# Attention and hard-swish MLP on one core: q and k transposed side by side by DMA and set apart by VectorE, decay rows from DRAM for all pairs

## The chip, the cores and the metric

The kernel runs on one core of a Trainium2 chip. The metric is device time in microseconds (us). Before the change, three runs gave a median of 357.02 us (356.66 to 357.11).

## The reference

Attention with a cumulative decay over 8 batches, 8 heads, 576 tokens and a head size of 64, and then an MLP with a hard-swish over all 4608 tokens. Cut to what matters:

```python
def attn(q, k, v, s):                       # q, k, v: 8 x 8 x 576 x 64, s: 8 x 8 x 576
    scores = (1 / 8) * q @ k^T              # 8 = sqrt(64)
    cum = cumsum(maximum(s, 0), axis=-1)
    bias = -(cum[:, :, :, None] - cum[:, :, None, :])
    scores = where(above the diagonal, -1e9, scores + minimum(bias, 0))
    return softmax(scores) @ v

x = attn(...) as (batch, token) rows of 8 heads x 64          # 4608 x 512
h = x @ w_in                                                  # 512 -> 2048
out = (h * clip(h + 3, 0, 6) / 6) @ w_out                     # 2048 -> 512
```

## The kernel before, in words

**Pairs and slots.** The 64 heads are taken two at a time: 32 pairs (p), each with 1152 tokens (2 x 576, the constant W2), which are 9 blocks of 128 (NTR). Everything that a pair needs lies in one of three slots (NS = 3, slot p % 3): qkT holds the transposed q and k side by side, v_h the values in f16. Scores are made as keys x queries: one operand is a 128-column block of kT, the other a stretch of qT, and the contraction runs over 128 partitions. The first 64 are the head's dimensions. Partitions 64 to 67 carry the decay: rows of the cumulative sum, in three f16 pieces, so that the product adds cum of the key minus cum of the query. Partitions 68 to 127 are mask rows: groups of ten tokens, with a large negative number for keys in later groups. So the scores come out of one matmul with decay and most of the mask. ScalarE takes the exponential from PSUM into Pm (L358), GpSimd zeroes the triangles of the blocks on the diagonal (affine_select, L363), TensorE multiplies by v_h (attend, L438), and VectorE divides (L448, L450). x_transpose turns the result for the MLP, on TensorE for some pairs (L476 with the copy L484) and by a DMA transpose for most pairs from 8 on (L468).

**How q and k get into the slots.** Three ways, by pair:
- Pairs 0 to 4 (FIRST = 4): turn_first. GpSimd or ScalarE casts q and k into x0 next to their decay columns (L792), TensorE transposes 68 columns at a time (L798), a copy puts 68 rows into the slot (L804).
- Pairs 5 to 9 (up to PTD = 10): cast_qk casts on GpSimd (L243), transpose_group turns 5 and then 4 blocks on TensorE (L302) and VectorE copies q's and k's 64 rows (L317). The four decay rows come by load_aug (L236) from a DRAM scratch that store_aug wrote (L599, 10 heads). The mask rows stay in the slot from the pair before.
- Pairs 10 to 31: cast_columns on GpSimd builds xb with 18 blocks of 128 columns, 9 for q and 9 for k. Each block has 64 columns of the cast (L282), four decay columns (L285, L286) and 60 mask columns. transpose_dma turns all 18 blocks by one DMA transpose straight into the slot, all 128 partitions (L291). The mask columns of the two xb buffers are filled once (copy_columns, L253) from a constant that load_columns brings from DRAM (L249). The decay columns come from decay_columns (27 TensorE transposes, L261, and a VectorE copy, L269) and decay_order (four GpSimd copies, L276).

**Order.** The schedule is written by hand: each engine works through its instructions in program order and waits in place. SyncE issues nearly all DMAs: loads of q, k (L210) and v (L224, L228), load_aug, transposes and results (L565). GpSimd issues the weight loads. A small fence DMA (L898) holds pair 4's loads back until a chunk of w_out has landed.

The first 8 heads run by themselves. Then comes the first MLP block, and with it decay_scan, decay_rows (GpSimd, L149 to L155), store_aug, the fence and the loads of pairs 4, 5 and 6. second_pair runs pairs 4 to 8, with tasks of the MLP put between; it loads pair p + 3 and casts for pair p + 1, and for pair p + 2 from 10 on. Its flag early (p > FIRST + 2) decides whether the cast and the first transpose group of pair p + 1 come ahead of x_transpose and attend or behind. From pair 9 on, att_tasks lists a pair's tasks (loads; the scores banks of the even and the odd head, s0 and s1; casts; attends) with costs, and weave puts them between the MLP's tasks in proportion. Tasks of cost 0 ride along.

**PSUM.** The MLP's first matmul (m1, L508) fills a 512-column bank, ScalarE clips it from below into trl (L518), VectorE multiplies trl, clipped from above, with the bank into gT (L519). Only then is the bank free. m1 has two banks in turn (3 and 4), in block 1 also bank 5 for every third group, and the second matmul (m2, L551) mostly bank 5, emptied by VectorE (L563).

Of the kernel before, what the change touches and what calls it, by code (L numbers as in the profile page):

```python
# [10 lines left out]
F16 = mybir.dt.float16  # L11
# [5 lines left out]
def kernel(  # L17
# [10 lines left out]
    nc = tc.nc  # L28

    B, H, SEQ, D = q.shape  # L30
    NH = B * H
# [35 lines left out]
    def pair_of_banks(b):  # L67
# [12 lines left out]
        name="sums",  # L80
    )

    gran = np.arange(SEQ) // GRAN
    rows = np.arange(60)
    amask_np = np.ones((2, 64, SEQ), dtype=np.float16)
    amask_np[0, 4:64] = gran[None, :] == rows[:, None]
    amask_np[1, 4:64] = np.where(gran[None, :] < rows[:, None], -16384.0, 0.0)
    row = np.arange(W2).reshape(NTR, 128).T % SEQ
    xaug_np = np.concatenate([amask_np[1][:, row], amask_np[0][:, row]], axis=2)
    xaug_dram = nc.inline_tensor(  # L90
        np.ascontiguousarray(xaug_np.transpose(1, 2, 0)).reshape(128, 2 * NTR * 64),
        name="xaug",
    )

    NA = 2 * (PTD - COLS)
    aug_dram = nc.dram_tensor("aug_scratch", (2, 4, NA * SEQ), F16, kind="Internal").ap()

    fence_dram = nc.dram_tensor("fence", (1, 32), F16, kind="Internal").ap()

# [6 lines left out]
    v_f = cpool.tile([128, NS, 2, 5, D], F32, tag="c_vf")  # L106
    v_h = cpool.tile([128, NS, 2, 5, VS], F16, tag="c_vh")
    Pm = cpool.tile([128, NS, PW], F16, tag="c_P")
    xb = cpool.tile([128, 2, 2 * NTR, 128], F16, tag="c_xb")
    dec = cpool.tile([128, NTR, 3, NP], F16, tag="c_dec")  # L110
    dec_f = cpool.tile([128, 3, NTR * NH], F16, tag="c_decf")
    xT = cpool.tile([128, KC, NT + 64], F16, tag="c_xT")
    warm = cpool.tile([128, 512], F16, tag="c_warm")
    one = cpool.tile([128, 2], F16, tag="c_one")
# [21 lines left out]
    wrap = work.tile([NH, 3, 128], F16, tag="wrap", bufs=1)  # L136

    def decay_scan():
        nc.vector.tensor_scalar(
# [6 lines left out]
    def decay_rows():  # L146
        r1 = work.tile([NH, SEQ], F32, tag="s0", bufs=1)
        g = nc.gpsimd
        g.tensor_copy(out=kaug[:, 0, :], in_=c8)  # L149
        nc.scalar.activation(out=qaug, in_=c8, func=AF.Copy, scale=-1.0)  # L150
        g.tensor_tensor(out=r1, in0=c8, in1=kaug[:, 0, :], op=ALU.subtract)
        g.tensor_copy(out=kaug[:, 1, :], in_=r1)
        g.tensor_tensor(out=kaug[:, 2, :], in0=r1, in1=kaug[:, 1, :], op=ALU.subtract)
        g.tensor_copy(out=wrap[:, :, 0:64], in_=kaug[:, 0:3, 512:SEQ])
        g.tensor_copy(out=wrap[:, :, 64:128], in_=kaug[:, 0:3, 0:64])  # L155

    def select(view, pattern, base, step, fill, src=None):
        nc.gpsimd.affine_select(
# [73 lines left out]

    def load_aug(p, eng):
        sl = p % NS
        c0 = (p - COLS) * W2
        eng.dma_start(  # L236
            out=qkT[64:68, sl, 0:2 * W2].rearrange("r (i c) -> r i c", i=2),
            in_=aug_dram[:, :, c0:c0 + W2].rearrange("i r c -> r i c"),
        )
# [3 lines left out]
        nc.gpsimd.tensor_copy(out=t, in_=qk_f.pop(p))  # L243
        qk_h[p] = t

    xaug = cpool.tile([128, 2 * NTR, 64], F16, tag="c_xaug")

    def load_columns():
        nc.sync.dma_start(out=xaug.rearrange("p t c -> p (t c)"), in_=xaug_dram.ap())  # L249

    def copy_columns(i, half):
        t = slice(half * NTR, (half + 1) * NTR)
        nc.vector.tensor_copy(out=xb[:, i, t, 64:128], in_=xaug[:, t, :])  # L253

    def decay_columns():
        pD = f16(pair_of_banks(6), 3 * NTR * NH)
        for i in range(3):
            for t in range(NTR):
                n = i * NTR + t
                c = 128 * t if t < 4 else 64 + 128 * (t - 5)  # L260
                nc.tensor.matmul(  # L261
                    out=pD[:, n * NH:(n + 1) * NH],
                    lhsT=wrap[:, i, :] if t == 4 else kaug[:, i, c:c + 128],
                    rhs=ident[0:NH, 0:NH],
                    is_transpose=True,
                    start=(n % 16 == 0),
                    stop=(n % 16 == 15 or n == 3 * NTR - 1),
                )
        nc.vector.tensor_copy(out=dec_f.rearrange("p i c -> p (i c)"), in_=pD)  # L269

    def decay_order():
        dv = dec_f.rearrange("p i (t a h) -> p t i a h", t=NTR, h=2)
        for r0, r1, j0, j1, h in (
            (0, 128, 0, 4, 0), (0, 64, 4, 5, 0), (64, 128, 4, 5, 1), (0, 128, 5, 9, 1)
        ):
            nc.gpsimd.tensor_copy(  # L276
                out=dec[r0:r1, j0:j1, :, :], in_=dv[r0:r1, j0:j1, :, :, h]
            )

    def cast_columns(p):  # L280
        x = xb[:, p % 2]
        nc.gpsimd.tensor_copy(  # L282
            out=x.rearrange("p (i t) c -> p t i c", i=2)[:, :, :, 0:D], in_=qk_f.pop(p)
        )
        nc.gpsimd.tensor_copy(out=x[:, NTR:2 * NTR, D:D + 3], in_=dec[:, :, :, p])  # L285
        nc.gpsimd.tensor_scalar_mul(  # L286
            out=x[:, 0:NTR, D + 3:D + 4], in0=dec[:, :, 0:1, p], scalar1=-1.0
        )

    def transpose_dma(p):  # L290
        nc.sync.dma_start(  # L291
            out=qkT[:, p % NS, 0:2 * W2].rearrange("p (t c) -> p t c", c=128),
            in_=xb[:, p % 2].rearrange("p t c -> p (t c)"),
            transpose=True,
        )

    def cast_v(p):
        sl = p % NS
# [315 lines left out]
    def att_tasks(p):  # L614


        more = p + 1 < NP

        def loads():
            if p + 3 < NP:  # L620
                load_pair(p + 3)
            if p < PTD - 1:
                cast_qk(p + 1)

        def casts():
# [12 lines left out]
        late = [(lambda: attend(2 * p - 1), 600 if PTD <= p < PTD + 3 else 1200)]  # L638
        back = []
        if p > FIRST:  # L640
            back = [(lambda: x_transpose(p - 1), 0 if by_dma(p - 1) else 640)]
        a = [(loads, 0)]
        if p <= PXD:
            a += scores(2 * p) + tr[0] + late
            a += scores(2 * p + 1) + [(casts, 0)] + tr[1] + back
        else:
            s0, s1 = scores(2 * p), scores(2 * p + 1)
            a = late + (back + a if by_dma(p - 1) else a + s0[:2] + back)
            a += (s0 if by_dma(p - 1) else s0[2:]) + tr[0]
            if p == PXD + 1:  # L650
                for half in range(2):
                    s1.insert(2 * half, (lambda half=half: copy_columns(1, half), 0))
            a += s1 + [(casts, 0)] + tr[1]
        return a, [(lambda: attend(2 * p), 1800 if PTD <= p + 1 < PTD + 3 else 1200)]

    def second_pair(p, fill):
        s0, s1, v = scores(2 * p), scores(2 * p + 1), values(2 * p)
        first = p == FIRST

        def more(n=1):  # L660
            run(fill[:n])
# [36 lines left out]
        if p + 3 < PTD:  # L698
            load_aug(p + 3, nc.sync)
        cast_v(p + 1)  # L700
        if PTD <= p + 2:
            cast_columns(p + 2)
            transpose_dma(p + 2)
        more()

# [269 lines left out]
```

## Time and profile before

| | |
|---|---|
| timed runs | 357.02 us median (356.66 to 357.11) |
| profiled execution, whole | 358.79 us |
| its span, first to last instruction | 357.0 us |
| granted TensorE clock | 1.00 |
| VectorE L519, 144 of 128x512 | 98.0 us, 686 ns each |
| TensorE L508 and L551, 512 columns | 143.3 and 138.9 us, 379 ns each |
| TensorE L261, decay transposes | 27 instructions |
| GpSimd L282, L285, L286, 22 each | 1147, 227 and 281 ns each |
| DMA transposes qkT<-xb, 22 | 4.7 us to landing (median), 2.8 us on SyncE |
| DMA transposes xT<-xs, 18 | 2.6 us to landing (median), 1.24 us on SyncE |
| store aug_scratch<-aug | 1, 90.0 KB |
| load xaug<-xaug | 1, 288.0 KB |
| loads qkT<-aug_scratch | 5, 18.0 KB each |

How to read it: busy time is what an engine's instructions cover; the idle time before a group of instructions is put down to what came last. A wait counts for the kernel only if TensorE, which is never long without work here, waits in the end. In the timeline, a row starts with start and duration in us, and xN counts like instructions merged into it; SPq is SyncE's queue of DMA issues.

### The profile page before, as it was taken

Reading aid. Unit: us, or ns where it says so; the run is one execution under the profiler, and the core shown is the slowest. Engines: PE = TensorE matmul, PEld = TensorE weight load, DVE = VectorE, ACT = ScalarE, POOL = GpSimd, SP = SyncE. Lnnn points to the kernel's source line nnn. Section 1 sums busy time; section 2 is a strip of 40 time slices with the busy share of each in tenths; the row PEclk is TensorE's granted clock in tenths of the full one; section 3 lists DMA queues with packets and bytes.
Section 4 is the critical chain, followed back from the end, with each engine's and each line's share of the span. In section 5 each row is a group of like instructions: output and inputs, shape, how many; then the busy total and the mean of one; then the engine's idle time right before and its main releaser. Section 6 shows DMA issues by size and latency. Waiting matters only on the chain.

```text
span 357.0 us, 7691 instructions
## 1 busy us (share of the span) xinstructions
PE 347.0 (97%) x2858; PEld 202.0 (57%) x2858; DVE 183.2 (51%) x314; ACT 208.0 (58%) x391; POOL 153.9 (43%) x371
## 2 busy tenths in 40 slices
PE   7999999999999999999999999999999999999995
PEld 3775566666555565655555555555555545444444
DVE  4758647787424563455345543544255635644531
ACT  4766456678646784777467755776478614534400
POOL 7695367754654555554445544454553200000000
PEclk9999999999999999999999999999999999999999
DMA  8999989899999999999998999999947110000012
GB/s 184 209 184 215 224 201 221 210 223 190 206 202 242 195 190 236 228 207 194 198 249 175 205 202 219 169 209 209 219 84 116 51 59 30 31 29 29 32 67 80
DMA packets 185389, 59.12 MB, mean 166 GB/s; under 512 B 177616, under 2 KB 180128, under 8 KB 185352
## 3 DMA queue, kind: packets, MB, share of 16 engines
q1 hardware_dynamic: 181720, 54.06, 70.2%
q0 software_dynamic: 2688, 4.19, 6.6%
q8 instruction: 22, 0.36, 0.4%
q10 hardware_dynamic: 944, 0.39, 0.4%
q14 instruction: 15, 0.12, 0.1%
HBM read 37.36 MB, written 9.53 MB: 131 GB/s over the span
## 4 chain that ended last, share of the span: by engine, by line
PE 82%; DMA 8%; DVE 3%; POOL 2%; ACT 1%; issue 1%; SPq 1%; POOLq 0%
PE PS L508 34%; PE PS L551 31%; PE PS L351 9%; PE PS L438 6%; DMA qkf<-in_k_dram 4%; DMA w_in<-in_moe_w_in_dram 2%; DMA qkT<-xb 2%; DVE qkT L317 1%; PE PS L574 1%; DVE gT L519 1%; ACT trl L518 1%; PE PS L476 1%; SPq L210 1%; POOL t L243 1%; POOL gT L792 1%
## 5 line engine op out<-in xcount | busy, mean ns | idle before, releaser
L519 DVE SCALAR_TENSOR_TENSOR gT<-trl,PS 128x512 f16<-128x512 f32 x144 | 98.0, 686 | 97.1 <-ACT trl L518 96.7
L508 PE MATMUL PS<-xT,w_in 128*128 128x512 f16 x576 | 143.3, 379 | 1.3 <-DVE gT L519 0.7
L518 ACT ACTIVATE trl<-PS,bias 128x512 f32<-128x512 f32 x144 | 98.7, 693 | 75.0 <-PE PS L508 73.2
L551 PE MATMUL PS<-w_out_sb,gT 128*128 128x512 f16 x560 | 138.9, 379 | 0.5 <-DVE osb L563 0.5
L358 ACT ACTIVATE Pm<-PS 128x384 f16<-128x384 f32 x224 | 102.7, 507 | 49.0 <-PE PS L351 46.8
L363 POOL TENSOR_SCALAR_AFFINE_SELECT Pm<-Pm 128x256 f16<-128x256 f16 x224 | 68.6, 308 | 109.3 <-ACT Pm L358 101.4
L508 PEld LDWEIGHTS <-w_in 128*128 128x128 f16 x576 | 60.9, 113 | 46.8 <-issue 2.4
L551 PEld LDWEIGHTS <-gT 128*128 128x128 f16 x560 | 51.4, 98 | 48.5 <-issue 0.7
L351 PE MATMUL PS<-qkT 128*128 128x256 f16 x392 | 61.8, 261 | 0.8 <-DMA qkT<-xb 0.6
L351 PEld LDWEIGHTS <-qkT 128*128 128x128 f16 x392 | 35.7, 98 | 31.3 <-DVE qkT L317 1.7
L438 PEld LDWEIGHTS <-Pm 128*128 128x128 f16 x960 | 37.5, 97 | 10.8 <-issue 0.3
L563 DVE TENSOR_SCALAR osb<-PS 128x512 f32<-128x512 f32 x35 | 24.1, 689 | 36.0 <-PE PS L551 35.8
L438 PE MATMUL PS<-v_h,Pm 128*128 128x65 f16 x960 | 40.4, 193 | 0.2
L450 DVE TENSOR_TENSOR xs<-PS,r 128x640 f16<-128x640 f32 x32 | 26.4, 825 | 1.1
L282 POOL CAST xb<-qkf 128x1152 f16<-128x1152 f32 x22 | 25.2, 1147 | 1.2 <-DMA qkf<-in_k_dram 1.2
L299 POOL CAST v_h<-v_f 128x640 f16<-128x640 f32 x32 | 23.0, 719 | 3.6 <-DMA v_f<-in_v_dram 3.5
L422 ACT ACTIVATE Pm<-PS 128x896 f16<-128x896 f32 (+1 forms) x16 | 13.1, 836 | 4.7 <-PE PS L416 4.6
L317 DVE COPY qkT<-PS 64x640 f16<-64x640 f16 (+1 forms) x20 | 9.1, 454 | 7.3 <-PE PS L302 7.0
L448 DVE RECIPROCAL r<-PS 128x10 f32<-128x10 f32 x32 | 6.9, 217 | 8.7 <-PE PS L438 8.3
L804 DVE COPY qkT<-PS 68x1152 f16<-68x1152 f16 (+2 forms) x13 | 7.5, 588 | 6.2 <-PE PS L798 6.1
L484 DVE COPY xT<-PS 128x576 f16<-128x576 f16 x14 | 6.4, 456 | 7.2 <-PE PS L476 6.0
L416 PE MATMUL PS<-qkT 128*128 128x64 f16 (+4 forms) x48 | 9.0, 277 | 0.6 <-DVE qkT L804 0.4
(74 smaller groups left out, 118.1 us busy)
## 6 DMA issues: line engine op xcount, KB each, us to landing
out_dram<-osb SPq DMA_DIRECT2D x35, 256.0 KB, 2.4
qkf<-in_q_dram SPq DMA_DIRECT2D x31, 288.0 KB, 3.3
qkf<-in_k_dram SPq DMA_DIRECT2D x31, 288.0 KB, 3.8
v_f<-in_v_dram SPq DMA_DIRECT2D x64, 128.0 KB, 3.4
w_in<-in_moe_w_in_dram POOLq DMA_DIRECT2D x4, 512.0 KB, 9.3
w_out_sb<-in_moe_w_out_dram POOLq DMA_DIRECT2D x4, 512.0 KB, 15.6
v_f<-in_v_dram SPq DMA_DIRECT2D x32, 32.0 KB, 2.5
qkT<-xb SPq DMA_TRANSPOSE x22, 4.7
```

Source lines behind the costliest of these rows:

```text
L282: nc.gpsimd.tensor_copy(out=x.rearrange("p (i t) c -> p t i c", i=2)[:, :, :, 0:D], in_=qk_f.pop(p))
L299: nc.gpsimd.tensor_copy(out=v_h[:, sl, :, :, 0:D], in_=v_f[:, sl])
L351: nc.tensor.matmul(out=S[:, c:c + hi - lo], lhsT=kT[:, sl, off + 128 * kt:off + 128 * (kt + 1)], rhs=qT[:, sl, off + lo:off + hi], start=( ...
L358: nc.scalar.activation(out=P[:, p0:p0 + n], in_=S[:, 0:n], func=AF.Exp, scale=0.125, bias=0.0)
L363: nc.gpsimd.affine_select(out=view, in_=view, pattern=pattern, compare_op=ALU.is_ge, fill=0.0, base=0, channel_multiplier=-1,)
L438: nc.tensor.matmul(out=O[:, hh, qt * VW:qt * VW + D + 1], lhsT=P[:, c:c + 128], rhs=v_h[:, sl, hh, kt, 0:D + 1], start=(qt == 0), stop=(qt ...
L450: nc.vector.tensor_tensor(out=xs.rearrange("p t h d -> p h t d"), in0=Ov[:, :, :, 0:D], in1=r.to_broadcast([128, 2, 5, D]), op=ALU.mult,)
L508: nc.tensor.matmul(out=ph, lhsT=w_in_t[f // 4][:, kc, f % 4, :], rhs=xT[:, kc, n * 512:(n + 1) * 512], start=(kc == 0), stop=(kc == KC - 1),)
L518: nc.scalar.activation(out=trl, in_=ph, func=AF.Relu, bias=bias3[:, 0:1], scale=1.0)
L519: nc.vector.scalar_tensor_tensor(out=gT2[:, n % 2, f, :], in0=trl, scalar=6.0, in1=ph, op0=ALU.min, op1=ALU.mult)
L551: nc.tensor.matmul(out=po, lhsT=gT2[:, n % 2, f, t4 * 128:(t4 + 1) * 128], rhs=w_out_sb[:, f, :], start=(f == 0), stop=(f == NF - 1),)
L563: nc.vector.tensor_scalar_mul(out=osb, in0=pouts[n, t4], scalar1=1.0 / 6.0)
```

## The change

For pairs 10 to 31, cast_beside casts q and k into xb with q's and k's 64 columns side by side in one block of 128, so there are 9 blocks and no decay or mask columns. transpose_dma turns these into a tile of its own, turned (two buffers), with q in partitions 0 to 63 and k in 64 to 127. A new task, apart, has VectorE copy both into the slot's first 64 partitions (two copies of 64x1152 f16). It stands behind the second scores bank of the odd head of the pair before. The decay rows of every pair from 5 on come by load_aug, so store_aug writes all 64 heads. The mask rows stay in the slots. The constant, its load, copy_columns, decay_columns, decay_order, wrap, dec and dec_f are gone. In second_pair, early begins one pair later (p > FIRST + 3), and the condition on m2_result is rewritten so that it still runs for pairs 5 and 6. TensorE's order of instructions differs in two places: the 27 decay transposes are gone, and pair 8's first group of five transposes comes later.

```diff
-    xaug_dram = nc.inline_tensor(...)
-    NA = 2 * (PTD - COLS)
-    aug_dram = nc.dram_tensor("aug_scratch", (2, 4, NA * SEQ), F16, kind="Internal").ap()
+    aug_dram = nc.dram_tensor("aug_scratch", (2, 4, NH * SEQ), F16, kind="Internal").ap()
...
-    xb = cpool.tile([128, 2, 2 * NTR, 128], F16, tag="c_xb")
-    dec = cpool.tile([128, NTR, 3, NP], F16, tag="c_dec")
-    dec_f = cpool.tile([128, 3, NTR * NH], F16, tag="c_decf")
+    xb = cpool.tile([128, 2, NTR, 2, D], F16, tag="c_xb")
+    turned = cpool.tile([128, 2, W2], F16, tag="c_turned")
...
-        g.tensor_copy(out=wrap[:, :, 0:64], in_=kaug[:, 0:3, 512:SEQ])
-        g.tensor_copy(out=wrap[:, :, 64:128], in_=kaug[:, 0:3, 0:64])
...
-        c0 = (p - COLS) * W2
+        c0 = p * W2
...
-    def load_columns():
-    def copy_columns(i, half):
-    def decay_columns():
-    def decay_order():
-    def cast_columns(p):
+    def cast_beside(p):
+        nc.gpsimd.tensor_copy(out=xb[:, p % 2], in_=qk_f.pop(p))
 
     def transpose_dma(p):
         nc.sync.dma_start(
-            out=qkT[:, p % NS, 0:2 * W2].rearrange("p (t c) -> p t c", c=128),
-            in_=xb[:, p % 2].rearrange("p t c -> p (t c)"),
+            out=turned[:, p % 2, :].rearrange("p (t c) -> p t c", c=128),
+            in_=xb[:, p % 2].rearrange("p t i d -> p (t i d)"),
             transpose=True,
         )
+
+    def apart(p):
+        sl = p % NS
+        nc.vector.tensor_copy(out=qT[0:64, sl, :], in_=turned[0:64, p % 2, :])
+        nc.vector.tensor_copy(out=kT[0:64, sl, 0:W2], in_=turned[64:128, p % 2, :])
...
-            in_=aug[2 * COLS:2 * COLS + NA].rearrange("h i r t -> h (i r) t"),
+            in_=aug.rearrange("h i r t -> h (i r) t"),
...
-            if p + 3 < PTD:
+            if p + 3 < NP:
                 load_aug(p + 3, nc.sync)
             if PTD <= p + 2 < NP:
-                cast_columns(p + 2)
+                cast_beside(p + 2)
                 transpose_dma(p + 2)
...
-            if p == PXD + 1:
-                for half in range(2):
-                    s1.insert(2 * half, (lambda half=half: copy_columns(1, half), 0))
+            if PTD <= p + 1 < NP:
+                s1.insert(2, (lambda: apart(p + 1), 0))
...
-        early = p > FIRST + 2
+        early = p > FIRST + 3
         load_pair(p + 3)
-        if first:
-            load_columns()
...
-        if early:
-            copy_columns(0, p % 2)
...
-            if not first:
+            if FIRST < p < FIRST + 3:
                 m2_result(0, p - FIRST)
         run(s1[3:])
-        if p + 3 < PTD:
-            load_aug(p + 3, nc.sync)
+        load_aug(p + 3, nc.sync)
...
-    decay_columns()
-    decay_order()
```

More of the change, by code (lines that the diff above doesn't have):

```diff
@@ L81 @@
     )
[L83 to L93, printed above, removed]
-    NA = 2 * (PTD - COLS)
-    aug_dram = nc.dram_tensor("aug_scratch", (2, 4, NA * SEQ), F16, kind="Internal").ap()
+    aug_dram = nc.dram_tensor("aug_scratch", (2, 4, NH * SEQ), F16, kind="Internal").ap()
     fence_dram = nc.dram_tensor("fence", (1, 32), F16, kind="Internal").ap()
@@ L135 @@
     qaug, kaug = aug[:, 0, 3, :], aug[:, 1]
-    wrap = work.tile([NH, 3, 128], F16, tag="wrap", bufs=1)
     def decay_scan():
@@ L244, in cast_qk @@
         qk_h[p] = t
-    xaug = cpool.tile([128, 2 * NTR, 64], F16, tag="c_xaug")
-    def load_columns():
-        nc.sync.dma_start(out=xaug.rearrange("p t c -> p (t c)"), in_=xaug_dram.ap())
-    def copy_columns(i, half):
-        t = slice(half * NTR, (half + 1) * NTR)
-        nc.vector.tensor_copy(out=xb[:, i, t, 64:128], in_=xaug[:, t, :])
-    def decay_columns():
[L256 to L269, printed above, removed]
@@ L271, in decay_order @@
-    def decay_order():
[L272 to L278, printed above, removed]
-    def cast_columns(p):
[L281 to L288, printed above, removed]
+    def cast_beside(p):
+        nc.gpsimd.tensor_copy(out=xb[:, p % 2], in_=qk_f.pop(p))
@@ L694, in second_pair @@
             transpose_group(p + 1, 0)
-            if not first:
+            if FIRST < p < FIRST + 3:
                 m2_result(0, p - FIRST)
         run(s1[3:])
-        if p + 3 < PTD:
-            load_aug(p + 3, nc.sync)
+        load_aug(p + 3, nc.sync)
         cast_v(p + 1)
         if PTD <= p + 2:
-            cast_columns(p + 2)
+            cast_beside(p + 2)
             transpose_dma(p + 2)
```

## The prediction

> **What bounds the kernel now.** I read the page first (busy time, slices), then who waited for whom on TensorE, then timelines of the three places where TensorE waits for something the change touches.
>
> ```profile
> PE 347.0 (97%) x2858; PEld 202.0 (57%) x2858; DVE 183.2 (51%) x314; ACT 208.0 (58%) x391; POOL 153.9 (43%) x371
> ...
> PE   7999999999999999999999999999999999999995
> ...
> DMA  8999989899999999999998999999947110000012
> ```
>
> TensorE has work in every slice, and the DMA engines are nearly full for the first 29 slices (262 us). A busy TensorE can hide bubbles, since 512-column matmuls are shown at 379 ns but start every 216 ns (four in 0.86 us in the chain of work). So I looked for gaps between starts. They add up to about 15 us: some 6 before 30 us (startup), 6 between 30 and 125 us, 3 in the 230 us after that. From 130 us on, TensorE is full: only something that makes it wait can move that part. The waits of TensorE name two in the change's reach:
>
> ```profile
> PE PS L302 <- POOL t L243: 0.7, 1, 0.7
> PE PS L351 <- DMA qkT<-xb: 0.6, 1, 0.6
> ```
>
> Each happens once. The timeline places them, with the starts of the rows ahead of them:
>
> ```profile
> 64.94 0.55 PE L351 MATMUL PS<-qkT 128*128 128x256 f16 x4
> 66.23 0.45 PE L302 MATMUL PS<-idtri,t 128*128 128x128 f16 x5 [0.75 <-POOL t L243]
> ...
> 100.84 1.03 PE L551 MATMUL PS<-w_out_sb,gT 128*128 128x512 f16 x4
> 102.45 0.56 PE L351 MATMUL PS<-qkT 128*128 128x256 f16 x4 [0.58 <-DMA qkT<-xb]
> ```
>
> Start to start, beyond the streaming time of the matmul before: 0.9 us at 65 us (pair 8's k load and its GpSimd cast are late) and 0.75 us at 101 us (pair 12's DMA transpose is late). The third place is about 0.9 us of work, the 27 small transposes of decay_columns (a row of the chain of work), with a DMA-bound stretch right behind them (rows of the timeline):
>
> ```profile
> 38.17 0.89 PE PS L261 x27
> ```
>
> ```profile
> 42.85 0.66 POOL L792 CAST gT<-qkf 128x576 f16<-128x576 f32 x1 [0.61 <-DMA qkf<-in_q_dram]
> ...
> 44.20 0.67 PE L798 MATMUL PS<-idtri,gT 128*68 128x128 f16 x9
> ```
>
> GpSimd begins pair 4's q cast the moment the load lands (42.85, ends 43.51); TensorE uses it at 44.20, only 0.7 us later.
>
> **What the Trainium skill says.** "Perfetto Trace Analysis", section "Identifying the Most-Contended Engine": matmul busy time is not a good measure, because matmuls are pipelined. The 379 against 216 ns agree. "DMA: Bandwidth & Descriptors", section "Queues, rings and completion order": on one DMA engine the descriptors of one issuing queue are consumed in ring order. So on SyncE's queue a load stands behind a store issued before it; no row here contradicts that, and I use it for the bigger store. "SBUF — State Buffer", section "Who interferes with whom": an SBUF-to-SBUF VectorE copy in a two-port mode and a GpSimd instruction exclude each other. The four copies of this shape in the trace (L195, 64x1152 f16, SBUF to SBUF) took 449 to 643 ns; the two over 600 ns ran beside GpSimd casts, the other two beside none: it agrees, as a partial delay.
>
> **The change, part by part.** All sums are against the profiled span, 357.0 us; that execution took 358.79, so 1.8 us lie around the span. The median of the timed runs is 357.02, so I add the sum to the median.
>
> *decay_columns and decay_order go.* 27 transposes, 0.89 us of TensorE in the chain, plus 0.1 us of bubbles at their edges: -1.0 us of TensorE work. Also gone, beside TensorE: one VectorE copy (1.05), four VectorE fills of xb (4 x 0.44), GpSimd's wrap and ordering copies (0.68 + 1.60), and per DMA pair GpSimd's two small copies (227 + 281 ns).
>
> *The store grows, the mask load goes.* store_aug writes all 64 heads: 590 KB instead of 90 KB, ahead of pair 4's loads on the same queue. 0.50 MB more, at the 227 GB/s of 40 to 50 us, is 2.2 us; what goes out beside the last w_out chunks costs the loads nothing. Bounds 0.6 and 2.2, I take 1.2 us. Then pair 4's q cast ends at 43.51 + 1.2 = 44.7, while TensorE, 1.0 earlier, arrives at 43.2: it starts the transposes at 44.75 instead of 44.20, so TensorE is 0.55 us late and the 1.0 is gone. Behind them k (cast end 44.73 + 1.2 against 45.57 + 0.55) fits. The DMA engines have about 2 us of room between 51 and 55 us, so the backlog doesn't last. In exchange load_columns (288 KB, 0.59 us of SyncE at 57.8) is gone, just ahead of pair 8's loads.
>
> *Pair 8's transposes move.* With early at p > FIRST + 3, the first transpose group of pair 8 comes after x_transpose, attend and one scores bank, which is 0.28 + 0.46 + 0.3 us of TensorE later, and its loads land no later than before. The 0.9 us stall at 65 us goes: from 0.55 late to 0.35 early.
>
> *DMA transposes halve, VectorE sets apart.* 22 transposes of 18 blocks (median 4.7 us to land, 2.8 us of SyncE) become 9 blocks. The 5-block ones of xT land in 2.6 us and hold SyncE for 1.24; the line between gives 3.25 us and 1.7 us for 9. VectorE then does two 64x1152 copies per pair, 0.45 to 0.64 us each from L195: I take 1.1 us for the two, bounds 0.9 and 2.4 (a 1.15 us GpSimd cast holding one of them off). SyncE also issues one load_aug of 18 KB per pair, 0.28 to 0.46 us each, ahead of the transpose. It waits for pair p's scores, the cast behind it waits for their masks, so its wait is covered; with 1.1 us less per transpose SyncE gains 0.7 us a pair. The transposes queued behind it, the xT transposes and the loads come earlier, not later.
>
> Whether 1.1 us of VectorE costs anything depends on the gap where it stands. In the changed order the copies for pair p + 1 follow the second scores bank of pair p's odd head. From pair 16 on, the gaps there are of this kind:
>
> ```profile
> 160.91 0.69 DVE L519 SCALAR_TENSOR_TENSOR gT<-trl,PS 128x512 f16<-128x512 f32 x1 [0.76 <-ACT trl L518]
> 163.20 0.69 DVE L519 SCALAR_TENSOR_TENSOR gT<-trl,PS 128x512 f16<-128x512 f32 x1 [1.60 <-ACT trl L518]
> ```
>
> 1.6 us free (pair 19; 23, 27, 31 likewise), 1.7 for 18, 22, 26, 30, 2.5 to 3.8 for 17, 21, 25, 29. For 16, 1.2; for 20, 24, 28 only 0.6, but the L519 behind has 9 us until its PSUM bank is used again. The transposes were issued 6 to 8 us before. So zero, up to 1.6 us for the two. If that cover goes (over 2.3 us), about 0.2 us a pair.
>
> Pair 10 is the exception:
>
> ```profile
> 79.28 3.11 SPq L291 DMA_TRANSPOSE qkT<-xb  x1
> ...
> 81.62 0.69 DVE L519 SCALAR_TENSOR_TENSOR gT<-trl,PS 128x512 f16<-128x512 f32 x1
> ...
> 82.00 2.76 PE L508 MATMUL PS<-xT,w_in 128*128 128x512 f16 x12
> ...
> 82.65 0.69 DVE L519 SCALAR_TENSOR_TENSOR gT<-trl,PS 128x512 f16<-128x512 f32 x1 [0.34 <-ACT trl L518]
> ```
>
> SyncE is behind here: the cast was ready at 77.1, the transpose goes out at 79.28. After: minus 0.66 (load_columns and its issue gap), plus two load_aug (0.37 each), so 79.35 to 79.5, landing at 82.7. The copies stand after the L519 that ends at 82.31, wait until 82.7, end at 83.8. Queued behind them on VectorE is the L519 of 82.65, then done at 84.5; its bank is what the third group of the row at 82.00 writes (82.00 + 2 x 0.86 = 83.73). TensorE waits until 84.5, 0.8 us later than before, whether it came 0.35 early or not.
>
> *Pair 12.* Its transpose (96.04, landing about 99.3) and copies (100.4) are done before 101.49, in a 4.2 us VectorE gap. The 0.75 us wait goes.
>
> Sum: the wait at pair 10 sets +0.8, pair 12 gives -0.75: +0.05, with 0.1 for small collisions at pairs 14 and 15 +0.15. 357.02 + 0.15 = 357.2 us.
>
> **The rivals.**
> *Slower: pair 10's transpose lands late and VectorE stands still.* One mechanism: VectorE is in order, so until it lands no PSUM bank is freed, and each us of delay is one of TensorE. If SyncE keeps the store's 1.2 us until 79 us, issue is 80.6, landing 83.9, copies to 85.0, L519 to 85.7: +2.0 - 0.75 = +1.2, 358.2 us. It decides above 0.2% from a landing after 83.3. For it: SyncE issues without pause from 58 to 79 us. Against: the room in the DMA at 51 to 55.
> *Slower in the steady part: copies and GpSimd block each other.* At over 2.3 us a pair, 0.2 us for most of 15 pairs less the gains, about +2: 359.0. For: the 643 ns copy. Against: gaps of 1.6 us.
> *Faster:* the transpose lands before 82.0 and copies take 0.45: the copies run 82.0 to 82.9 (TensorE is 0.35 early), L519 ends at 83.6, so -0.1 - 0.75 = -0.85, 356.2 us. For: nothing else is late then. Against: SyncE's row of issues.
> That the change doesn't do what it says is excluded: the work is visibly taken out.
>
> **Chances.** About 0.2% (0.7 us) is what can be told from no change. Forecast 357.2, own range 356.4 to 357.7: 0.41. Late landing 0.32, steady blocking 0.10, so slower 0.42. Faster 0.17. 8 in 10: 356.0 to 359.0, from the faster case to the worst one.
>
> **What would show it.** No L261 rows and 0.9 us less TensorE work; the pair-4 transposes later than 44.2 by about half a us behind a DMA wait; no wait for GpSimd at pair 8; a VectorE wait for the turned tile near 82 us and an L519-bank wait of TensorE there; no DMA wait near 101; 44 copies of 0.45 to 0.65 us without new TensorE waits after 130 us. TensorE waits of 0.2 us or more in every pair after 130 us, or a load at 40 us that isn't later, would make the prediction wrong.

## The result, and the profile after

The changed kernel takes 359.81 us (median of 8 runs, 358.36 to 361.80), the kernel before 357.06 us in the same session (8 runs, 356.66 to 357.58): a ratio of 1.0075, 95% interval 1.0049 to 1.0102. It is slower by 2.7 us. The forecast was 357.2 us, with a range of 356.0 to 359.0.

The eight runs fall into two groups by the clock that TensorE was granted over the whole run. Four at 1.00 took 358.36, 358.68, 358.72 and 359.34 us (the last is the profiled one). Three at 0.995 took 360.28 to 360.59, one at 0.989 took 361.80. So there are two things to explain: about 1.6 us at full clock (the median of the four is 358.70), and about 2 us more in half of the runs. The profiled execution of before took 358.79 us, more than each of its eight timed runs, so the two profiles lie closer together than the medians.

The page of the profiled execution (span 357.6 us, clock 1.00) is shown for the lines that answer to those of before.

```profile
PE 346.4 (97%) x2831; PEld 201.3 (56%) x2831; DVE 200.1 (56%) x353; ACT 208.0 (58%) x391; POOL 148.8 (42%) x321
...
PE   7999889999999999999999999999999999999996
...
DMA  8999999998798789897978888689923110010012
```

Most of what was to go is gone: 27 TensorE transposes, 50 GpSimd instructions, and of the time of 16 DMA engines a good part (SyncE's queue falls from 70.2% to 62.1%). VectorE is busy for 17 us more. New in TensorE's slices are the two 8s, at 36 to 54 us.

Of TensorE's waits, those of before for pair 8's cast and pair 12's transposed tile are no longer there. Two new ones are, of 0.9 us for the last chunk of w_out and of 1.9 us for pair 4's cast. The timeline of TensorE places both (start, length, work; in brackets the idle time ahead of the row and what ended it; L498 is L551 of before, L739 is L798):

```profile
39.62 2.75 PE L498 MATMUL PS<-w_out_sb,gT 128*128 128x512 f16 x12
43.23 1.02 PE L498 MATMUL PS<-w_out_sb,gT 128*128 128x512 f16 x4 [0.86 <-DMA w_out_sb<-in_moe_w_out_dram]
46.15 0.69 PE L739 MATMUL PS<-idtri,gT 128*68 128x128 f16 x9 [1.89 <-POOL gT L733]
```

Before, the 16 matmuls of the first two rows ran without a break:

```profile
40.75 3.62 PE L551 MATMUL PS<-w_out_sb,gT 128*128 128x512 f16 x16
```

And GpSimd's timeline gives the cast that the second one waits for:

```profile
45.43 0.66 POOL L733 CAST gT<-qkf 128x576 f16<-128x576 f32 x1 [10.90 <-DMA qkf<-in_q_dram]
```

Pair 4's transposes start at 46.15 instead of 44.20, although TensorE now arrives a microsecond earlier. q is cast at 45.43 instead of 42.85, 2.58 us later: its load is issued 0.43 us later (40.09 instead of 39.66), behind the fence, and takes 2.15 us more from issue to cast. The last chunk of w_out is late too: its records end at 42.8 us, 41.5 before. Start to start, TensorE stands still for 1.02 us at 42.0 and for 2.05 us at 43.9. The first of the two costs nothing by itself: the four matmuls that waited for w_out are through 2 us before q is cast.

From there on I compared when each group of 16 w_in matmuls starts (L508 before, L455 after) in the two profiles. After minus before is -0.1 us at 25 to 36 us, +1.55 at 72, +1.73 at 86, +1.22 at 109, and +1.18 for every group from 128 us to the last at 334 us. So in these two profiles, both at full clock, all of the loss arises between 40 and 54 us; 0.4 us of it is given back by 72 us and 0.5 us between 86 and 109, and nothing happens in the steady part. The span is only 0.6 us longer, since the stretch from the end of the last output packet to the end of the program is 1.36 us instead of 1.93.

### The profile page after: what moved, and what is told of

It reads as the page before. It is cut to its first block, busy times and chain, and to the rows that moved or that the text cites. A ratio compares the mean times of both kernels' runs of the same rounds, so it can differ in the third digit from the quotient of the medians.

```text
span 357.6 us, 7671 instructions
## 1 busy us (share of the span) xinstructions
PE 346.4 (97%) x2831; PEld 201.3 (56%) x2831; DVE 200.1 (56%) x353; ACT 208.0 (58%) x391; POOL 148.8 (42%) x321
## 3 DMA queue, kind: packets, MB, share of 16 engines
q1 hardware_dynamic: 156934, 48.18, 62.1%
## 4 chain that ended last, share of the span: by engine, by line
PE 78%; DMA 9%; DVE 6%; POOL 3%; issue 1%; ACT 1%; SPq 1%; POOLq 0%
PE PS L498 30%; PE PS L455 30%; PE PS L298 9%; PE PS L385 6%; DMA w_out_sb<-in_moe_w_out_dram 5%; DMA qkf<-in_k_dram 3%; DVE qkT L264 2%; DMA qkf<-in_q_dram 1%; DVE xs L397 1%; DVE gT L466 1%; PE PS L521 1%; ACT trl L465 1%; PE PS L423 1%; POOL w_in L437 1%; PE PS L249 1%
## 5 line engine op out<-in xcount | busy, mean ns | idle before, releaser
L455 PE MATMUL PS<-xT,w_in 128*128 128x512 f16 x576 | 143.3, 379 | 1.0 <-DVE gT L466 0.7
L498 PE MATMUL PS<-w_out_sb,gT 128*128 128x512 f16 x560 | 139.0, 379 | 1.3 <-DMA w_out_sb<-in_moe_w_out_dram 0.9
L310 POOL TENSOR_SCALAR_AFFINE_SELECT Pm<-Pm 128x256 f16<-128x256 f16 x224 | 73.0, 328 | 114.1 <-ACT Pm L305 104.9
L455 PEld LDWEIGHTS <-w_in 128*128 128x128 f16 x576 | 61.1, 113 | 46.5 <-issue 2.7
L498 PEld LDWEIGHTS <-gT 128*128 128x128 f16 x560 | 51.4, 98 | 49.5 <-issue 1.8
L246 POOL CAST v_h<-v_f 128x640 f16<-128x640 f32 x32 | 25.1, 783 | 0.8 <-DMA v_f<-in_v_dram 0.8
L241 DVE COPY qkT<-turned 64x1152 f16<-64x1152 f16 x22 | 10.0, 453 | 4.3 <-DMA turned<-xb 4.3
L733 POOL CAST gT<-qkf 128x576 f16<-128x576 f32 (+1 forms) x10 | 6.1, 615 | 14.5 <-DMA qkf<-in_q_dram 12.8
L242 DVE COPY qkT<-turned 64x1152 f16<-64x1152 f16 x22 | 10.5, 479 | 0.3
```

Source lines behind the costliest of these rows:

```text
L246: nc.gpsimd.tensor_copy(out=v_h[:, sl, :, :, 0:D], in_=v_f[:, sl])
L310: nc.gpsimd.affine_select(out=view, in_=view, pattern=pattern, compare_op=ALU.is_ge, fill=0.0, base=0, channel_multiplier=-1,)
L455: nc.tensor.matmul(out=ph, lhsT=w_in_t[f // 4][:, kc, f % 4, :], rhs=xT[:, kc, n * 512:(n + 1) * 512], start=(kc == 0), stop=(kc == KC - 1),)
L498: nc.tensor.matmul(out=po, lhsT=gT2[:, n % 2, f, t4 * 128:(t4 + 1) * 128], rhs=w_out_sb[:, f, :], start=(f == 0), stop=(f == NF - 1),)
```

## The theory and its rival

Theory S: the whole loss is the store of 590 KB in front of pair 4's loads. It takes the time of the DMA engines from the last chunks of w_out beside it and from the loads behind it, TensorE runs dry for 2 to 3 us, and after such a gap its clock is lowered for a while in some runs.

Theory T, the rival: the parts that were changed cost it, that is the nine-block transposes with two VectorE copies behind them, or the moved casts, and the wait at pair 4 is a symptom only.

The experiments ran in four later sessions. In them the kernel before has medians of 358.3 to 358.5 us, with single runs from 356.8 to 361.2; ratios are against the runs of the same session.

## The experiments

**1. The store alone, in the kernel before** (e2_bigstore).

```
-    aug_dram = nc.dram_tensor("aug_scratch", (2, 4, NA * SEQ), F16, kind="Internal").ap()
+    aug_dram = nc.dram_tensor("aug_scratch", (2, 4, NH * SEQ), F16, kind="Internal").ap()
...
-        c0 = (p - COLS) * W2
+        c0 = p * W2
...
-            in_=aug[2 * COLS:2 * COLS + NA].rearrange("h i r t -> h (i r) t"),
+            in_=aug.rearrange("h i r t -> h (i r) t"),
```

> The kernel before, with nothing changed but the size of its store (all 64 heads, 590 KB instead of 92 KB, in the same place). Theory S: pair 4's q cast starts near 45.4 us instead of 42.85, TensorE waits 0.1 to 0.5 us for w_out and about 1.6 us for the cast, part of it given back at the wait of 65 us; span +0.7 to +1.8 us, and a clock under 1.00 in some runs, so 358 to 360 us. Rival V: the store is absorbed, 357 to 357.5 us, clock 1.00.

Measured: 360.47 us, ratio 1.0061 (1.0040 to 1.0082), a little above the range given. TensorE's waits in its profile (total us, times, longest):

```profile
PE PS L350 <- DMA qkT<-xb: 1.8, 2, 1.0
...
PE PS L797 <- POOL gT L791: 1.2, 1, 1.2
```

The store makes the kernel before slower by about as much as the whole change does. Pair 4's cast is waited for here too, but it comes at 44.24, 1.39 us later than before, where 45.4 was expected. Nor did the lower clock come: no run is under 0.998, which the kernel before shows as well. In the starts of the w_in groups only 0.5 us are lost up to 72 us, and 1.1 us more at two transposed tiles at 101 and 111 us, which in this kernel have 18 blocks. So this run shows what the store costs, and only in part the place where the changed kernel pays it.

**2. The changed kernel without the 500 KB** (e5_none). It leaves the decay rows of heads 20 to 63 out of the store, 500 KB; pairs from 10 on read those of pairs 5 to 9 in their place.

```
-            in_=aug.rearrange("h i r t -> h (i r) t"),
+            in_=aug[2 * COLS:2 * COLS + NA].rearrange("h i r t -> h (i r) t"),
...
-        c0 = p * W2
+        c0 = (p % COLS) * W2
```

> Part of the computation is left out: the pairs from 10 on take the decay rows of pairs 5 to 9, so the 500 KB of decay rows of heads 20 to 63 never go out; the loads of the rows stay. Theory S (the big store is the whole loss, through what lies behind and beside it): pair 4's q is cast at about 42.9 us as in the kernel before, the wait for the last w_out chunk goes, and no wait over 1 us is left between 42 and 46 us; with the short stalls at 65 and 101 us gone as well the ratio is 0.992 to 0.998 of the kernel before. Rival T (the nine-block transposes, the copies or the moved casts cost the time): the ratio stays at 1.003 or above, and the wait of 2 us at pair 4 alone goes.

Measured: 357.48 us, ratio 0.9975 (0.9963 to 0.9987). q is cast at 43.02, the wait for w_out is gone, TensorE's wait for the cast is 0.8 us, and no other wait over 0.5 us is left that was not there before. GpSimd's cast and TensorE's first transposes:

```profile
43.02 0.66 POOL L734 CAST gT<-qkf 128x576 f16<-128x576 f32 x1 [8.83 <-DMA qkf<-in_q_dram]
```

```profile
43.73 0.69 PE L740 MATMUL PS<-idtri,gT 128*68 128x128 f16 x9 [0.84 <-POOL gT L734]
```

All 22 runs have a clock of 0.999 or 1.00. All else of the change is in this kernel, and by the medians it is 0.9 us faster than the kernel before. Theory T falls. From here to the ratio of the changed kernel kept busy (1.0027, experiment 3, another session) the 500 KB cost 0.5%, 1.9 us, which fits the 2.2 us of experiment 1; with the lower clock (1.0045) it is 0.7%, 2.5 us.

**3. The changed kernel again, and with TensorE kept busy** (e4_again, e3_warm). e3_warm adds twelve matmuls whose results nobody reads into the gap:

```
-    run(fill[:4])
+    run(fill[:3])
+    keep_warm(4)
+    run(fill[3:4])
+    keep_warm(8)
```

> The changed kernel once more, unchanged, beside the others on this chip: median 358.4 to 361, clock 1.00 in some runs and 0.989 to 0.995 in others, the latter 1.8 to 3.5 us longer.

> The changed kernel with 12 dummy matmuls of 512 columns on TensorE where it waits at 42 to 46 us (4 ahead of the last quarter of the first m2 group, 8 behind it), so that it hardly stands still there; the loads come when they did. If the gap is what lowers the clock: clock 1.00 in all runs, spans of 356.5 to 357.8 as in the runs of the changed kernel at 1.00, time 358.3 to 359.4 with a small spread. If the lower clock comes from elsewhere: runs at 0.995 and below as before, median near 359.8.

Measured: unchanged 360.63 us (358.43 to 361.18), ratio 1.0045 (1.0027 to 1.0063); kept busy 359.49 us (358.94 to 360.12; up to 359.4 was expected), ratio 1.0027 (1.0013 to 1.0041). Of the 22 unchanged runs 13 have a clock of 0.994 or 0.995 and a median of 360.94, nine have 1.00 and 359.26. Of the 22 kept busy none is under 0.999. The unchanged kernel's profiled execution is one of those with the lower clock. It has one gap on TensorE, of 2.32 us from 43.6 us on, and no wait for w_out. The row that ends it, and the stretch behind it (window, length, then busy time and count of PE, PEld, DVE, ACT and POOL, the granted clock, the share of the DMA engines, GB/s):

```profile
46.09 0.69 PE L739 MATMUL PS<-idtri,gT 128*68 128x128 f16 x9 [2.16 <-POOL gT L733]
```

```profile
46.00:54.00 8.00, 7.81 (x59) 4.61 (x60) 2.32 (x5) 2.49 (x6) 3.85 (x9) 0.79 1.12 229
```

In the 8 us right behind the gap the clock is 0.79, and 59 matmuls are done where 72 are in the profile at full clock; from 36 to 46 and from 54 to 63 us it is 1.00. In the stretch from 46.7 to 50.1 us alone it is 0.50. Half the clock for 3.4 us is 1.7 us of work, which is the difference between the two groups of runs (360.94 and 359.26). "TensorE: Matmul & The Clock Gate" of the Trainium skill, section "Why this matters for your kernels", warns of idle gaps over about 3 us. This trace shows the drop after 2.3 us, and 13 of 22 runs have a mean that fits one such drop. Other profiles have gaps of 2.26 us (e8_double) and 2.86 us (e11_behind) and no drop behind them, so the length of the gap doesn't decide alone; what else does is open. The dummies cure it and leave the rest, about 0.3%: the late q itself.

**4. The store on ScalarE's queue** (e7_actq).

```
-    store_aug(nc.sync)
+    store_aug(nc.scalar)
```

> The store of 590 KB goes out at the same point on ScalarE's DMA queue in place of SyncE's, so that pair 4's q and k no longer stand behind it in one ring, but share the engines with it. If the order in the ring sets the delay, q is cast 1 to 2 us earlier than the changed kernel's 45.4 and k is late instead, ratio 1.000 to 1.003. If only the bytes count, q is cast at 45 or later and the ratio stays at 1.004 or above.

Measured: 359.18 us, ratio 1.0019 (1.0007 to 1.0031). q is cast at 45.51, no earlier than behind the store in the same ring. So in this place it isn't the order in the ring that delays q, but the bytes: the store's packets run from 38.6 to 44.0 us, as on SyncE's queue (38.4 to 43.8). The Trainium skill says so in "DMA: Bandwidth & Descriptors", section "Issuing engines are not separate DMA queues": whoever issues, the same 16 engines do the work. The ratio is still better than expected from that. TensorE's idle time is in two pieces here. The first is 1.49 us at 35 us: ScalarE, in program order, stands at the store until the decay rows are ready (it does nothing from 33.1 to 35.5 us but issue the store at 34.75). The second is 1.47 us at 45 us. All 22 runs have 0.999 or 1.00, and the loss is about that of the changed kernel kept busy (1.0019 and 1.0027).

**5. The store behind pair 4's loads** (e11_behind), and **cut in two** (e1_split, heads 10 to 19 in the old place and heads 20 to 63 behind the loads of pairs 4 to 6).

```
-    store_aug(nc.sync)
     nc.sync.dma_start(out=fence_dram, in_=w_out_sb[0:1, 11, 0:32])
     load_pair(FIRST)
+    store_aug(nc.sync)
```

> The whole store of 590 KB stands behind the loads of pair 4 instead of ahead of them. If the loss is only the delay of pair 4, q is cast at about 43 us, no wait is left at 42 to 46 us, ratio 0.997 to 1.000. If the DMA engines have no room before 70 us, as the run with the store cut at head 20 makes likely, the delay passes to pair 5 and 6 and to pair 10's turned tile: new waits of 1 to 2 us in all for a cast at 50 to 70 us or at 85 us, ratio 1.001 to 1.004.

```
-    store_aug(nc.sync)
+    store_aug(nc.sync, aug_dram, 2 * COLS, NE)
     nc.sync.dma_start(out=fence_dram, in_=w_out_sb[0:1, 11, 0:32])
     load_pair(FIRST)
     for p in range(COLS, COLS + 2):
         load_pair(p)
         load_aug(p, nc.sync)
+    store_aug(nc.sync, aug_late, NE, NH)
```

> The changed kernel with its store cut in two: the rows of pairs 5 to 9 go to DRAM where they did before (92 KB), the rows of pairs 10 to 31 in a second store, issued by SyncE behind the loads of pairs 4, 5 and 6. Theory S (the 590 KB store ahead of pair 4's loads is the whole loss: TensorE waits 1.0 us for w_out and 2.1 us for pair 4's q, and that gap brings the lower clock of some runs): both waits go, the clock is 1.00 in all runs, and the time falls below the kernel before, to 355.5 to 356.5 us. Rival V (the loss is what the VectorE copies and the extra DMAs do from pair 10 on): the waits at 42 to 46 us go but the median stays above 358.5. Rival C (the lower clock in some runs has nothing to do with that gap): runs at 0.995 stay, the median between 356 and 358.

Measured: behind pair 4, 361.22 us, ratio 1.0084 (1.0051 to 1.0117); cut in two, 360.05 us, ratio 1.0042 (1.0027 to 1.0058). Both are worse than expected; of the first, the case without room is right in kind, but a ratio of at most 1.004 was given for it. In it, pair 4's wait falls to 1.1 us, and TensorE then stands still for 2.86 us at 50.3 us, where GpSimd is late because it waited 2.56 us for pair 5's k; four of seven runs have the lower clock. In the second, one of 22 runs has it. Its median is above the 358.5 us that were given for rival V, but no cost of VectorE's copies in every pair shows: q is cast at 43.66 and w_out is not waited for. But the casts of the next pairs are waited for (0.9 us in two pieces), and pair 10's turned tile lands so late that TensorE loses 1.30 us at 85 us. The bytes find no room before 70 us: moving the store in front of other loads moves the loss.

**6. The late part where the DMA engines have room** (e6_late, e10_wide). Heads 10 to 25 stay in the old place, the rest goes out behind pair 11's DMA transpose at 87 us. In e6_late the late store takes heads 26 to 63, in e10_wide heads 16 to 63, of which the first ten are not read (NL = 16 stands for NE = 26 in the line below).

```
+        if p == PTD + 1:
+            store_aug(nc.sync, aug_late, NE, NH)
```

> The store is cut at head 26: heads 10 to 25 (147 KB) in the old place, heads 26 to 63 (350 KB) behind the DMA transpose of pair 11, at about 86 us. Theory S with room (from about 85 us the DMA engines are at 7 to 8 tenths in the changed kernel, and each load is there long before its cast): q of pair 4 is cast at 43.0 to 43.5, nothing waits behind the late store, ratio 0.993 to 0.999. Rival: 350 KB cost about 1.7 us of all engines wherever they go, as in the run with the store cut at head 20, and pair 12's or 13's turned tile lands too late: ratio 1.001 to 1.004, with a new TensorE wait between 90 and 110 us.

> As the run with the late store behind pair 11's transpose, but the late store takes 48 heads (16 to 63, 442 KB) in place of 38 (350 KB). The records of that run show on average two packets of the late store under way at a time, and 8.4 us from its first to its last; of the store of 64 heads up to 18 at a time. Theory W (the split of the rows over the DMA engines was at fault, 38 rows on two engines): with 48 heads the store is through in 1 to 2.5 us, the DMA transpose behind it holds SyncE's queue for 1.2 to 2.5 us in place of 5.7, and the ratio falls from 1.014 to 0.999 to 1.003. Rival (a DMA transpose always waits for a large store ahead of it on its ring, by its bytes): SyncE's queue is held for 5 us or more again, ratio 1.01 or above.

Measured: 38 heads 364.18 us, ratio 1.0142 (1.0099 to 1.0185); 48 heads 357.95 us, ratio 0.9994 (0.9979 to 1.0009). More bytes, 6 us less. The first is outside both expectations, the second within that of theory W. SyncE's queue in the first, right behind the late store (issued at 87.02):

```profile
87.93 5.68 SPq L419 DMA_TRANSPOSE xT<-xs  x1
```

and in the second (store issued at 86.75):

```profile
87.42 3.50 SPq L419 DMA_TRANSPOSE xT<-xs  x1
```

This row, a transpose that holds the queue for about 1.2 us in most places, holds it for 5.68 us (3.50 in the second, more than the 2.5 expected). All that follows on SyncE is late, and on VectorE's timeline the first copy of pair 12 waits 7.79 us for its tile:

```profile
104.88 0.45 DVE L245 COPY qkT<-turned 64x1152 f16<-64x1152 f16 x1 [7.79 <-DMA turned<-xb]
```

Meanwhile TensorE stands still for 3.45 us, and it has a clock of 0.74 from 107 to 116 us. In the DMA records the 304 packets of the store of 38 heads take from 88.3 to 96.7 us, 2.0 at a time on average; the 384 of 48 heads are through from 87.9 to 91.9, 9.4 at a time: 4.0 us, where theory W gave 1 to 2.5. That is the rule of the page "DMA: Bandwidth & Descriptors" in "Why a DMA increments its semaphore by 16 and not by 1": the number of engines is the largest up to 16 that divides the slowest dimension, so 2 for 38, 16 for 48 (and 10 for the 10 heads of the kernel before). These two runs agree. The number of bytes was not what made e6_late lose. Of e10_wide's late store nothing is seen on TensorE: against the kernel without the 500 KB its groups are 0.70 us later both at 72 us, before it, and at 109 us, after it.

**7. Three stores, and a small one** (e9_three, the later two at 63 and 105 us; e12_small, heads 20 to 25 behind pair 4's loads).

```
+        if p == FIRST + 1:
+            store_aug(nc.sync, aug_mid, 16, 32)
...
+        if p == PTD + 3:
+            store_aug(nc.sync, aug_late, 32, NH)
```

```
     load_pair(FIRST)
+    store_aug(nc.sync, aug_mid, 2 * PTD, NE)
```

> The decay rows go out in three stores: heads 10 to 19 in the old place as before the change, heads 16 to 31 (147 KB) behind the loads of pair 8 at about 59 us, heads 32 to 63 (295 KB) behind the DMA transpose of pair 13 at about 104 us. Theory S with room: nothing of it is waited for, the start is that of the run without the 500 KB (q of pair 4 cast at about 43 us), and the ratio is 0.996 to 0.999, at most 0.2% above that run. Rival: the bytes cost what they cost in any place, and a TensorE wait of more than 0.5 us for a cast near 70 us or for a turned tile near 85 or 110 us shows; ratio 1.001 to 1.005.

> As the run with 48 heads behind pair 11's transpose, but of the first store only heads 10 to 19 are left in the old place (as in the kernel before), and heads 20 to 25 (55 KB) go out behind the loads of pair 4. In that run the block at 72 us stands 0.7 us later than in the run without the 500 KB, and the late store itself adds nothing after that. Theory S: the 0.7 us are the 55 KB ahead of pair 4; behind its loads they are hidden, ratio 0.9970 to 0.9990, below both kernels. Rival (no room there either: pair 5's casts or pair 10's turned tile come later by what pair 4 gains): ratio 0.999 to 1.003, in the second case with a TensorE wait of 1.3 us for VectorE's gate near 84 us, as in the run with three stores.

Measured: three stores 358.52 us, ratio 0.9999 (0.9988 to 1.0010); the small one behind pair 4's loads (with 48 heads late, as in e10_wide) 358.49 us, ratio 1.0005 (0.9992 to 1.0018). Neither reaches the 0.9975 of the run without the bytes; both expectations of a gain are missed. In e9_three pair 4's wait is that of the run without the 500 KB (0.9 us), but the 147 KB at 63 us make pair 10's tile late. VectorE's timeline:

```profile
82.85 0.59 DVE L246 COPY qkT<-turned 64x1152 f16<-64x1152 f16 x1 [0.64 <-DMA turned<-xb]
83.46 0.88 DVE L247 COPY qkT<-turned 64x1152 f16<-64x1152 f16 x1
```

They begin 0.64 us late and take 0.56 us more than two copies elsewhere (GpSimd casts in these moments), and TensorE loses 1.3 us. In e12_small no such wait is left, and still nothing is won. The store behind pair 13 costs nothing. So of the places tried, those up to 70 us cost, and those from 87 us on are free as long as the store doesn't go out on 2 engines as in e6_late. e10_wide is better than the changed kernel by 0.5% and the intervals don't touch; from the kernel before it can't be told apart. None of the complete kernels is faster than the kernel before.

**8. The copies doubled** (e8_double).

```
-        nc.vector.tensor_copy(out=qT[0:64, sl, :], in_=turned[0:64, p % 2, :])
-        nc.vector.tensor_copy(out=kT[0:64, sl, 0:W2], in_=turned[64:128, p % 2, :])
+        for _ in range(2):
+            nc.vector.tensor_copy(out=qT[0:64, sl, :], in_=turned[0:64, p % 2, :])
+            nc.vector.tensor_copy(out=kT[0:64, sl, 0:W2], in_=turned[64:128, p % 2, :])
```

> Every copy that sets q and k apart is made twice, so VectorE has 44 more copies of about 0.45 us, 0.9 us more for each of 22 pairs. Theory H (in the steady part from pair 12 on the copies lie in gaps of VectorE): the trace shows the same distances between the blocks from 120 us to the end as without, at most 0.7 us is lost at pair 10, where VectorE has just met its gate work, and the time is 0 to 0.8 us above the changed kernel, 1.004 to 1.008 of the kernel before. Rival V (VectorE is close to its limit): each doubled pair delays TensorE by 0.1 us or more, together over 2 us.

Measured: 366.66 us, ratio 1.0240 (1.0212 to 1.0269). Theory H was far off, and V's "over 2 us" is right with much to spare: seen in the starts of the w_in groups, the doubled copies lose 7.5 us against the changed kernel between 82 and 260 us, mostly in steps of 0.3 to 1.4 us. One such step, on VectorE:

```profile
165.30 0.44 DVE L242 COPY qkT<-turned 64x1152 f16<-64x1152 f16 x1
165.77 0.46 DVE L243 COPY qkT<-turned 64x1152 f16<-64x1152 f16 x1
166.26 0.86 DVE L242 COPY qkT<-turned 64x1152 f16<-64x1152 f16 x1
167.15 1.29 DVE L243 COPY qkT<-turned 64x1152 f16<-64x1152 f16 x1
```

and on GpSimd at the same time:

```profile
165.86 0.95 POOL L247 CAST v_h<-v_f 128x640 f16<-128x640 f32 x1
166.76 1.38 POOL L230 CAST xb<-qkf 128x1152 f16<-128x1152 f32 x1
```

The first two copies end before GpSimd's casts begin. The added two fall on them and take 0.86 and 1.29 us. Over the kernel 12 of 88 copies take about 0.86 and eight about 1.29 us; in the changed kernel none of 44 takes over 0.57. This is the second rival of the prediction, copies and GpSimd holding each other up, called up by one more pair of copies. A pair's copies take 2.37 us here, and the loss is about 0.35 us a pair, where the prediction gave 0.2 for over 2.3 us. The prediction read gaps of 1.6 us for several pairs: 0.9 us of copies fit there, 1.8 do not. How much of the loss is the two more copies by themselves and how much their growth beside the casts, the run doesn't separate.

## Why the prediction was wrong, step by step

**The store: this step failed, by its size.** It said "0.50 MB more [...] is 2.2 us; what goes out beside the last w_out chunks costs the loads nothing. Bounds 0.6 and 2.2, I take 1.2 us." In the profile of after q is cast 2.58 us later, above the upper bound; in the other profiles with this store in this place of the changed kernel it is 2.52 (e4_again), 2.40 (e3_warm) and 1.92 us (e8_double), and in e2_bigstore 1.39. What failed is the microsecond that the step took off for bytes going out beside the w_out chunks. In the profile of after these chunks, on which the step put no price, end 1.3 us later; the fence, which waits for a chunk of them, lets q's load go 0.43 us later; and from issue to cast q takes 5.3 us instead of 3.2 (3.7 in e5_none, without the bytes). Which ring the store stands in makes no difference (e7_actq: q at 45.51). TensorE's own wait for w_out is not needed for the loss: it is 1.02 us in the profile of after and absent in e4_again, and pair 4's transposes start at 46.15 and 46.09. With the full 2.2 us for q the step's own sum gives a cast that ends at 45.7 (46.1 measured) and TensorE 1.55 us late, where it had 0.55 and the profile has 1.95.

**The clock: missing.** No step asked what TensorE's clock does after a gap of over 2 us. It was left at nothing without a reason. In the first session it adds about 2 us to half of the runs, and 1.1 us to the median of the eight (358.70 at full clock, 359.81 in all). Without it the time would lie between 356.0 and 359.0 and near the first rival's 358.2, but by another path: the delay is at pair 4, not at pair 10.

**Removal of decay_columns: right and worth nothing.** The rows are gone and TensorE arrives at pair 4 about 1 us earlier, to wait there, as the step said.

**"The backlog doesn't last": half right.** Beyond 54 us it is not seen in the changed kernel, where the loss even shrinks. But e11_behind, e1_split and e9_three show that there is no room to spare up to 70 us.

**Pair 8: right in kind.** The stall at 65 us is gone. 0.4 us were won between pair 4 and 72 us, where the step had 0.9.

**Transposes and copies: right.** The nine-block transpose holds SyncE for 1.33 us (median; 1.7 said) and lands about 3.4 us after its issue where the landing is seen, in e1_split and e9_three (3.25 said). A pair's two copies take 0.9 us (1.1 said). From 128 us on no more than a hundredth of a microsecond is lost by them.

**Pair 10: the wait did not come.** The forecast's sum rests on it: whatever came before, TensorE would end there 0.8 us late. It adds 0.18 us, on top of the 1.55 us that are left of the store's delay at 72 us. So the kernel is late, but not for the reason that the sum gave. SyncE issues pair 10's transpose at 78.72, about 2.2 us earlier against TensorE than the forecast had it, and VectorE finds the tile there (its timeline, a gate row and the copies):

```profile
83.17 0.69 DVE L466 SCALAR_TENSOR_TENSOR gT<-trl,PS 128x512 f16<-128x512 f32 x1 [0.76 <-ACT trl L465]
83.78 0.45 DVE L241 COPY qkT<-turned 64x1152 f16<-64x1152 f16 x1
84.24 0.46 DVE L242 COPY qkT<-turned 64x1152 f16<-64x1152 f16 x1
```

The step counted SyncE's issues and took their lengths from before. Those of the loads got shorter (the two v loads at 60 us hold the queue for 2.95 us together before, 1.65 after). That fewer bytes are on the way then is the likely reason; no run tested it. The first rival, pair 10's tile late and VectorE standing still, does occur in e1_split and e9_three, at a cost of 1.3 us. In the changed kernel it doesn't.

**Pair 12: right.** Its wait is gone, and 0.5 us are won between 86 and 109 us (0.75 said).

What is left open: why the clock falls in some runs and not in others. Also why the program ends 0.57 us sooner after its last output packet: the kernel before and e2_bigstore have 1.9 us there, ten profiles of kernels built on the changed one 1.26 to 1.36, e9_three and e12_small 1.70, and no run took it apart. And 55 KB more ahead of pair 4 or right behind it (e10_wide, e12_small) seem to cost 0.6 to 0.7 us by 72 us against e5_none, more than their bytes; but e9_three, with the old store there, is as late. Single profiles differ by up to 1.0 us at their first groups, and that of e5_none took 356.87 us against a median of 357.48, that of e9_three 359.32 against 358.52, so this is not settled.

## What to carry to other kernels

Where the DMA engines are full, price a new transfer by all of its bytes for everything that is due in that stretch, on whatever queue, and ask for each waiting engine which of the loads it waits for first; then look for a stretch with room, and store there only what is due later. Behind a stall of 2 us or more on TensorE look for a second price, a lower clock for the next microseconds, and look in many runs: it came in 13 of 22 here. And for a gap that hides a VectorE copy, look also at when GpSimd's next cast begins, not only at VectorE's own next instruction.

## What the runs showed of the hardware that was not expected

- The clock of TensorE can fall after a gap of 2.3 us: to 0.50 for 3.4 us, 0.79 over the 8 us behind the gap in the profiled execution, with a mean of 0.994 or 0.995 over the run in 13 of 22 runs. It need not: profiles with gaps of 2.26 us (e8_double) and 2.86 us (e11_behind) kept 1.00. Gaps of 1.5 us, even twice (e7_actq), left it at 0.999 or 1.00 in all 22.
- A store of 38 rows went out 2 packets at a time and held a DMA transpose behind it on SyncE for 5.68 us; 48 rows, 26% more bytes, were through in 4.0 instead of 8.4 us.
- A copy of 64x1152 f16 on VectorE takes 0.45 us alone and 0.86 or 1.29 us beside GpSimd's casts, which grow at the same time from 0.72 to 0.95 and from 1.15 to 1.38 us.
